# Attention and top-1 experts in one kernel: masks in two 64-row parts, a new order for attention, and the experts' first product inside that order

## The chip, the core and the metric

The kernel runs on one core of a Trainium2 chip. The metric is the device time of one execution in microseconds; the time before is the median of three runs. The engines are TensorE (PE; its weight loads are PEld), VectorE (DVE), ScalarE (ACT), GpSimd (POOL) and SyncE (SP), which starts most transfers.

## What is computed

Attention over 8 batches of 8 heads, 576 positions, head size 64, with a decay made of a running sum of logarithms, and then a mixture of 8 experts in which each token goes to one expert:

```python
scores = scale * np.matmul(q, k.transpose(0, 1, 3, 2))
cum = np.cumsum(np.log(np.clip(f, 0.0001, 1.0)), axis=-1)
scores = np.where(causal, -1e9, scores + cum[:, :, :, None] - cum[:, :, None, :])
attn = np.exp(scores - np.max(scores, axis=-1, keepdims=True))
x = (attn / (attn.sum(-1, keepdims=True) + 1e-9)) @ v        # then (4608, 512)
logits = x @ w_gate + modality_bias[modality_id]
e_idx = np.argmax(logits, axis=1)                             # gate_w: its softmax
out[mask] = gate_w[mask, None] * (np.maximum(x[mask] @ w1[e], 0.0) @ w2[e])
```

## The kernel before, in words

**Attention** takes two heads at a time, one in rows 0 to 63 of TensorE and one in rows 64 to 127: 32 pairs, four to a batch. The work of a pair p is cut into named steps. `raw`, `hi`, `lo` load and split q and k into X (the X split of GpSimd is L335). `mm` 0 to 2 compute scores for the row maxima (`max_mm`): first the causal mask is put into the PSUM bank by matmuls of a 128-row identity with a mask (L419), then come the products of X (L424) and of the decay's row (L428) with 64 rows, one matmul for each head. `mr` reduces them on VectorE (L438, L440, L443) into `mt`. `sp` transposes `mt` on TensorE (L449), `ssp` splits it on VectorE (L455, L456), `so` writes it by a transfer into Sq (L463). `s` 0 to 3 compute the shifted, masked scores (`scores`: mask L480, products L492), `e` takes their exponential on ScalarE (L502, into Pt), `h` rounds Pt to Ph on ScalarE (L513), and `r` forms the remainder Pl (L521; GpSimd, one of three on VectorE). `w` is the weighted sum with v for one head, 45 matmuls into a single bank `po` (L541 to L543), and `d` divides it on VectorE (L552 to L554) into x. `gt`, `gc`, `gm`, `ga` transpose x (L568), copy it to xT (L573), multiply by the gate (L584) and add (L590). When a batch is whole, `rt` 0 to 8 route its tokens (`route`): maximum, first expert that attains it (L602 rd, L606 and L607 rc, L610 rei), one-hot (L612, L615 roh), ranks by a small matmul, running counts (L633 acc), the destination row of every token (L640 rde), and scattering transfers of the tokens into `xs` from GpSimd (L653).

**The order of attention** is a list. `steps` describes every step with its engines, estimated durations, rings of buffers and a due time, which is the pair's number times PER plus an entry of the table DUE. `Plan.order` is a list scheduler that always takes the step that can start first, ties by due time, and the instructions of all engines are written in that order under a manual schedule. One step, `early`, makes the experts' first tables and loads the first two tiles of tokens once batch 5 is routed.

**The experts** work on tiles of 256 tokens, 21 full tiles and then half tiles (`Moe.run`). `prepare` transposes a tile's tokens (L989) and splits them into xh, xl (L991, L992). `first(t)` forms x times w1 in four groups of 24 matmuls (L1003) and splits the result into hh, hl (L1006). `second(t)` multiplies by w2 in 48 matmuls (L1014). `split_w1` and `split_w2` split the loaded weights, high half on ScalarE (L969, L976), low half on VectorE (L970, L977); L957 and L963 load them. At tile 1 `other_tables` makes the remaining tables, some 52 small VectorE instructions that follow from the last batch's counts (c_acc is L1137). Before the change all of this is written behind attention, and a scheduler orders it.

## Time and profile before

| what | us |
|---|---|
| median of three runs (lowest, highest) | 1004.14 (994.04, 1006.01) |
| the profiled execution: its time | 1013.86 |
| its span in the trace | 1012.1 |
| TensorE matmuls, busy | 927.0 (92%), 9347 instructions |
| VectorE, busy | 684.1 (68%) |
| ScalarE, busy | 537.5 (53%) |
| GpSimd, busy | 361.6 (36%) |
| mean granted TensorE clock | 0.938 |

Start times are counted from the span's start. A matmul's own duration is longer than its distance to the next, since matmuls overlap; distances of starts are what adds up. In a row with a bracket, the bracket gives the idle time ahead of the instruction and what ended it. The granted clock is a share of full speed.

### The profile page before, as it was taken

How to read it: one execution, taken by the hardware profiler on the slowest of the kernel's cores; microseconds unless marked ns; L12 is line 12 of the kernel's file. 1: busy time of each engine (PE TensorE's matmuls, PEld its weight loads, DVE VectorE, ACT ScalarE, POOL GpSimd, SP SyncE). 2: the span in 40 equal slices, each digit the busy share in tenths (PEclk: the TensorE clock that was granted, in tenths of full speed). 3: DMA queues.
4: the chain of work that ended last, by engine and by line, in shares of the span. 5: the costliest groups of instructions: out<-in, count | busy, mean ns of one | idle time of the engine just before them, and what ended most of it. 6: DMA issues, size and time to landing. Idle time of an engine off the chain costs nothing. (4 is left out here: it accounts for less than half of the span.)

```text
span 1012.1 us, 22740 instructions
## 1 busy us (share of the span) xinstructions
PE 927.0 (92%) x9347; PEld 808.8 (80%) x9347; DVE 684.1 (68%) x1173; ACT 537.5 (53%) x655; POOL 361.6 (36%) x278
## 2 busy tenths in 40 slices
PE   5999989999999899979689999999999999999792
PEld 3787778777778777768588999999999999999571
DVE  7867978686777858777547766566666666665382
ACT  2765656655756547547443444445444544544371
POOL 7454556865566474653424311111111110111010
PEclk9897999998999969989779999999999999999796
DMA  5212132332321322212302676111111441124640
GB/s 180 77 50 99 33 126 67 99 99 74 97 78 53 99 84 89 87 57 86 131 33 79 218 256 235 43 43 42 53 43 53 134 139 55 43 84 168 234 161 3
DMA packets 38276, 98.22 MB, mean 97 GB/s; under 512 B 3919, under 2 KB 4559, under 8 KB 38160
## 3 DMA queue, kind: packets, MB, share of 16 engines
q1 hardware_dynamic: 31456, 75.60, 22.5%
q0 software_dynamic: 6704, 21.02, 5.5%
q8 instruction: 79, 1.29, 0.6%
q14 instruction: 37, 0.30, 0.1%
HBM read 133.69 MB, written 21.80 MB: 154 GB/s over the span
## 5 line engine op out<-in xcount | busy, mean ns | idle before, releaser
L521 POOL TENSOR_TENSOR Pl<-Pt,Ph 128x1152 f16<-128x1152 f32 (+1 forms) x64 | 152.3, 2385 | 156.2 <-ACT Ph L513 104.4
L502 ACT ACTIVATE Pt<-ps,lnp 128x1024 f32<-128x1024 f32 (+1 forms) x128 | 117.2, 928 | 112.8 <-PE ps L492 104.8
L1017 POOL DMA_INDIRECT out_dram<-y,xg x36 | 47.4, 1316 | 349.4 <-DVE y L1016 333.1
L1003 PE MATMUL ph<-xh,w1h 128*128 128x256 f32 x576 | 164.3, 286 | 2.0 <-ACT xh L991 1.5
L1003 PE MATMUL ph<-xl,w1h 128*128 128x256 f32 x576 | 164.3, 285 | 0.0
L1003 PE MATMUL ph<-xh,w1l 128*128 128x256 f32 x576 | 164.1, 285 | 0.0
L976 ACT CAST w2h<-raw 128x1024 fp32r<-128x1024 f32 x84 | 86.6, 1050 | 115.1 <-PE py L1014 84.7
L970 DVE TENSOR_TENSOR w1l<-raw,w1h 128x1024 fp32r<-128x1024 f32 x80 | 100.9, 1265 | 58.1 <-ACT w1h L969 57.7
L977 DVE TENSOR_TENSOR w2l<-raw,w2h 128x1024 fp32r<-128x1024 f32 x84 | 100.3, 1221 | 56.5 <-ACT w2h L976 55.2
L969 ACT CAST w1h<-raw 128x1024 fp32r<-128x1024 f32 x80 | 83.3, 1048 | 95.6 <-PE ph L1003 57.8
L492 PE MATMUL ps<-X 64*128 64x288 f32 (+4 forms) x1152 | 125.8, 327 | 0.0
L1014 PE MATMUL py<-w2h,hh 128*128 128x512 f32 x312 | 121.6, 398 | 0.0
L1014 PE MATMUL py<-w2l,hh 128*128 128x512 f32 x312 | 119.7, 391 | 0.7 <-DVE w2l L977 0.7
L1014 PE MATMUL py<-w2h,hl 128*128 128x512 f32 x312 | 119.5, 392 | 0.0
L513 ACT CAST Ph<-Pt 128x1024 f16<-128x1024 f32 (+1 forms) x96 | 103.7, 1082 | 21.3 <-PE po L543 20.3
L1003 PEld LDWEIGHTS ph<-xh,w1h 128*128 128x128 f32 x576 | 111.5, 194 | 3.6 <-ACT xh L991 2.4
L1003 PEld LDWEIGHTS ph<-xl,w1h 128*128 128x128 f32 x576 | 111.7, 194 | 0.7
L541 PE MATMUL po<-vh,Ph 128*128 128x65 f16 x960 | 104.9, 202 | 7.5 <-DVE x L554 7.5
L1003 PEld LDWEIGHTS ph<-xh,w1l 128*128 128x128 f32 x576 | 111.7, 194 | 0.0
L543 PE MATMUL po<-vh,Pl 128*128 128x65 f16 x960 | 104.7, 201 | 5.0 <-issue 3.5
L542 PE MATMUL po<-vl,Ph 128*128 128x64 f16 x960 | 104.8, 200 | 1.8 <-issue 1.8
L492 PEld LDWEIGHTS ps<-X 64*128 64x128 f32 x1152 | 93.1, 196 | 13.2 <-issue 1.8
(253 smaller groups left out, 2025.7 us busy)
## 6 DMA issues: line engine op xcount, KB each, us to landing
raw<-in_w_dram SPq DMA_DIRECT2D x84, 1024.0 KB
raw<-in_qk_dram SPq DMA_DIRECT2D x32, 608.0 KB
xg<-xs SPq DMA_DIRECT2D x20, 514.0 KB
vr<-in_v_dram SPq DMA_DIRECT2D x7, 1024.0 KB
raw1b<-in_w_dram SPq DMA_DIRECT2D x4, 1024.0 KB
hxg<-xs SPq DMA_DIRECT2D x5, 257.0 KB
vr<-in_v_dram SPq DMA_DIRECT2D x2, 512.0 KB
vr<-in_v_dram SPq DMA_DIRECT2D x8, 128.0 KB
```

What stands on the lines that cost most here:

```text
L492: nc.tensor.matmul(ps[:, h, c0:c0 + w], a, b, start=(j == 0 and not masked), stop=(j == 3), skip_group_check=True)
L502: nc.scalar.activation(self.get("Pt", (p, i))[:, :, o:o + w], ps[:, :, 0:w], AF.Exp, bias=self.lnp, scale=0.125)
L513: self.nc.scalar.copy(self.Ph_t[p % 2][:, :, c], self.get("Pt", (p, i))[:, :, 0:c.stop - c.start])
L521: e.tensor_tensor(self.Pl_t[p % 2][:, :, c], self.get("Pt", (p, i))[:, :, 0:c.stop - c.start], self.Ph_t[p % 2][:, :, c], ALU.subtract)
L541: nc.tensor.matmul(o, Ph[:, c0:c0 + P], vh[:, c, hh, :], start=(c == 0), stop=False)
L542: nc.tensor.matmul(o[:, 1:65], Ph[:, c0:c0 + P], vl[:, c, hh, :], start=False, stop=False)
L543: nc.tensor.matmul(o, Pl[:, c0:c0 + P], vh[:, c, hh, :], start=False, stop=(c == ic))
L970: nc.vector.tensor_tensor(self.w1l[a], self.raw1[i][a], f32(self.w1h[a]), ALU.subtract)
L976: nc.scalar.copy(self.w2h[a], self.raw2[a])
L977: nc.vector.tensor_tensor(self.w2l[a], self.raw2[a], f32(self.w2h[a]), ALU.subtract)
L1003: nc.tensor.matmul(ph[:, i, :], w[:, k, f0:f0 + P], x[:, k, :], start=(j == 0), stop=(j == len(m) - 1))
L1014: nc.tensor.matmul(py, h[:, k, c * P:c * P + P], w[:, k, :], start=(j == 0), stop=(j == len(m) - 1))
```

## The change

1. **Masks.** The identity of 128 rows gives way to `id2`, and the masks `after` and `later` get a second plane, so that a mask is put in by matmuls of 64 rows, one for each head, as the products are. A segment wider than 64 takes two parts, one 128 columns wide and one 64 wide. A pair of heads had 20 mask matmuls and has 36.
2. **The order.** PER is 13.0 instead of 13.5, DUE has other numbers, and the step costs are given anew.
3. **Route.** L602, L606, L607 and L633 move from VectorE to GpSimd; L640 becomes three GpSimd operations.
4. **The experts' tile 0.** Loading w1 (`mw1`), tokens (`mx`) and w2 (`mw2`), splitting w1 (`ms`), `prepare` of tiles 0 and 1 (`mp`) and `first(0)` (`mf`) are steps of attention's list. For that a part of attention's buffers is closed at `mopen` and `mps`, inside the list, and the experts' tiles are opened in four pieces.

```diff
-PER = 13.5
+PER = 13.0
...
-    ('setup2',): 36.45, ('hi',): -18.87, ('lo',): -67.23, ('cum',): -14.17, ('mm', 0): -2.46, ('mm', 1): -11.48,
+    ('setup2',): 205.22, ('hi',): -34.14, ('lo',): 184.6, ('cum',): 237.26, ('mm', 0): -559.83, ('mm', 1): 5.51,
...
+        self.soon, self.soon_ps = ctx.enter_context(ExitStack()), ctx.enter_context(ExitStack())
+        pool = lambda name, bufs=1, **kw: (ctx if "side" in kw else self.soon).enter_context(tc.tile_pool(name=name, bufs=bufs, **kw))
+        self.ps_o = pool("a_o", space=PSUM, side="right")
+        self.ps_b = pool("a_b", space=PSUM, side="right")
+        self.ps_s = self.soon_ps.enter_context(tc.tile_pool(name="a_s", bufs=3, space=PSUM))
...
-        self.ident16 = t([P, P], BF16, "ident16")
-        self.later = t([P, P], BF16, "later")
-        self.after = t([P, P], BF16, "after")
-        nc.vector.tensor_copy(self.ident16, self.ident)
-        nc.gpsimd.memset(self.after, 0.0)
-        nc.gpsimd.affine_select(self.after, self.after, [[-1, P]], ALU.is_ge, -BIG, base=0, channel_multiplier=1)
+        self.id2 = t([P, 2, P], BF16, "id2")
+        self.later = t([P, 2, P], BF16, "later")
+        self.after = t([P, 2, P], BF16, "after")
+        nc.gpsimd.memset(self.id2, 0.0)
+        for x in range(2):
+            nc.vector.tensor_tensor(self.id2[:, x, 64 * x:64 * x + 64], self.ident[:, 0:64], self.ident[:, 64:P], ALU.add)
+        def mask(t, k):
+            nc.gpsimd.memset(t, 0.0)
+            for h in range(2):
+                a = t[64 * h:64 * h + 64]
+                nc.gpsimd.affine_select(a, a, [[64 * k, 2], [-k, P]], ALU.is_ge, -BIG, base=0, channel_multiplier=k)
+        mask(self.after, 1)
...
-        for h in range(2):
-            for j, (c0, w, ic, j0) in enumerate(masked):
-                n = min(w, P)
-                nc.tensor.matmul(pm[:, h, c0 + w - n:c0 + w], self.ident16, self.after[:, P - n:], start=(j == 0), stop=False,
-                                 skip_group_check=True)
+        first = True
+        for c0, w, ic, j0 in masked:
+            for x, n in ((0, P), (1, 64)) if w > 64 else ((1, 64),):
+                for h in range(2):
+                    r = slice(64 * h, 64 * h + 64)
+                    nc.tensor.matmul(pm[:, h, c0 + w - n:c0 + w], self.id2[r, x], self.after[r, x, P - n:], start=first, stop=False,
+                                     skip_group_check=True)
+                first = False
...
+        for c0, w, c, i0 in masked:
+            for x, n in ((1, P), (0, 64)) if w > 64 else ((0, 64),):
+                for h in range(2):
+                    r = slice(64 * h, 64 * h + 64)
+                    nc.tensor.matmul(ps[:, h, c0:c0 + n], self.id2[r, x], self.later[r, x, 0:n], start=first, stop=False,
+                                     skip_group_check=True)
+                first = False
...
-            nc.vector.tensor_tensor(d, lg, m.broadcast_to(s3), ALU.subtract)
+            nc.gpsimd.tensor_tensor(d, lg, m.broadcast_to(s3), ALU.subtract)
...
-            nc.vector.tensor_scalar(c, self.get("rd", b), 0.0, 8.0, ALU.is_lt, ALU.mult)
-            nc.vector.tensor_tensor(c, c, self.iota_e, ALU.add)
+            nc.gpsimd.tensor_scalar(c, self.get("rd", b), 0.0, 8.0, ALU.is_lt, ALU.mult)
+            nc.gpsimd.tensor_tensor(c, c, self.iota_e, ALU.add)
...
-            nc.vector.tensor_tensor(na, self.get("rtot", b), self.acc, ALU.add)
+            nc.gpsimd.tensor_tensor(na, self.get("rtot", b), self.acc, ALU.add)
...
-            nc.vector.scalar_tensor_tensor(de, self.get("rei", b), float(CAP), r1, ALU.mult, ALU.add)
+            e0 = sm.tile([P, NJ, 1], F32, name="re0")
+            nc.gpsimd.tensor_scalar(e0, self.get("rei", b), float(CAP), None, ALU.mult)
+            nc.gpsimd.tensor_tensor(e0, e0, r1, ALU.add)
+            nc.gpsimd.tensor_copy(de, e0)
...
+            last = [("s", n - 1, g) for g in range(4)] + [("vl", nb - 1, c) for c in range(NJ)]
+            add("mw1", (), "SP", 1.1, lambda: moe.load_w1(moe.row[0]), (), [("early",)], d, lands=2.1e6)
+            add("mopen", (), "SP", 0.0, lambda: (self.soon.close(), moe.open_left()), (), last, d)
+            for x in range(2):
+                add("mx", (x,), "SP", 0.4, lambda x: moe.load_x(x), (x,), [("mopen",)], d, lands=527e3)
+            add("mps", (), "SP", 0.0, lambda: (self.soon_ps.close(), moe.open_banks()), (), [("e", n - 1, g) for g in range(4)] + [("mopen",)], d)
+            add("mw2", (), "SP", 1.1, lambda: moe.load_w2(), (), [("mw1",), ("mopen",)], d, lands=2.1e6)
+            for q in range(4):
+                add("ms", (q,), [("ACT", 1.05), ("DVE", 1.25)], 0, lambda q: moe.split_w1(0, [q]), (q,), [("mw1",), ("mopen",)], d + q)
+            for x in range(4):
+                add("mp", (x,), [("PE", 0.6), ("ACT", 0.6), ("DVE", 0.7)], 0, lambda x: moe.prepare(x // 2, [x % 2]), (x,), [("mps",), ("mp", x - 1), ("mx", x // 2)],
+                    d + x)
+            for g in range(4):
+                add("mf", (g,), [("PE", 2.9), ("ACT", 0.75), ("DVE", 0.75)], 0, lambda g: moe.first(0, [g]), (g,),
+                    [("mp", 1), ("ms", g)], d + 1 + g, take=("ph", g), free=[("ph", g)])
...
-        self.load_w1(self.row[0])
-        self.load_w2()
-        self.split_w1()
         self.nc.gpsimd.memset(self.raw1[1], 0.0)
-        self.prepare(0)
...
-                self.first(t)
+                if t:
+                    self.first(t)
                 self.split_w1()
-                if t + 1 < FULL:
+                if 1 < t + 1 < FULL:
                     self.prepare(t + 1)
...
+        moe.open_rest()
+        moe.run(acc)
```

The places at which the instructions move, first **TensorE at a score group**, the masks ahead of 288-wide products (ident and id are the identities, later the mask, mt the maxima). Before:

```order
L449 MATMUL pb<-ident,mt 10x128
L480 LDWEIGHTS ident_162
L480 MATMUL ps<-later,ident_162 128x128
L480 LDWEIGHTS ident_162
L480 MATMUL ps<-later,ident_162 128x128
L480 LDWEIGHTS ident_162
L480 MATMUL ps<-later,ident_162 128x128
L480 LDWEIGHTS ident_162
L480 MATMUL ps<-later,ident_162 128x128
L492 MATMUL ps<-X 128x320 x6
L492 MATMUL ps<-Sq,Sk 128x320 x2
```

and after (L495 is the mask, L508 the product):

```order
L495 LDWEIGHTS id_163
L495 MATMUL ps<-later,id_163 128x128
L495 LDWEIGHTS id_163
L495 MATMUL ps<-later,id_163 128x128
L495 LDWEIGHTS id_163
L495 MATMUL ps<-later,id_163 128x64
L495 LDWEIGHTS id_163
L495 MATMUL ps<-later,id_163 128x64
L508 MATMUL ps<-X 128x288 x6
L508 MATMUL ps<-Sq,Sk 128x288 x2
```

A segment's mask is now four matmuls of 64 rows; from the mask to the products the number of rows stays the same.

Second, **a batch's route**. On VectorE before, between the reductions of the maxima (lg are the logits, rm their maximum):

```order
L438 TENSOR_REDUCE mt<-ps 128x2 x2
L590 TENSOR_TENSOR lg<-pb,lg 128x40
L600 TENSOR_REDUCE rm<-lg 128x5
L602 TENSOR_TENSOR rd<-lg,rm 128x40
L606 TENSOR_SCALAR rc<-rd 128x40
L607 TENSOR_TENSOR rc<-rc,iota_e 128x40
L440 TENSOR_REDUCE ps<-ps 128x2
L610 TENSOR_REDUCE rei<-rc 128x5
```

and on GpSimd after, between the remainders Pl and the split of X (L345):

```order
L537 TENSOR_TENSOR Pl_199<-Pt,Ph_197 128x2x576
L618 TENSOR_TENSOR rd<-lg,rm 128x40
L622 TENSOR_SCALAR rc<-rd 128x40
L623 TENSOR_TENSOR rc<-rc,iota_e 128x40
L345 TENSOR_TENSOR X<-raw,X 128x1216
L537 TENSOR_TENSOR Pl_199<-Pt,Ph_197 128x2x512
L649 TENSOR_TENSOR acc<-rtot,acc 128x8
L537 TENSOR_TENSOR Pl_198<-Pt,Ph_196 128x2x576
L657 TENSOR_SCALAR re_4845<-rei 128x5
L658 TENSOR_TENSOR re_4845<-re_4845,rr_4842 128x5
L659 CAST rde<-re_4845 128x5
```

Seven small operations of each batch have gone from VectorE's queue to GpSimd's.

Third, **the hand-over**. ScalarE after, from the last copies of the gates (xT) to the first tile's tokens (xh); raw holds weights as loaded:

```order
L589 COPY xT<-pb 128x512
L676 ACTIVATE rex<-rd 128x40
L1022 CAST w1h<-raw_78 128x4x256 x2
L1029 CAST w2h<-raw_9091 128x1024 x4
L589 COPY xT<-pb 128x128
L1022 CAST w1h<-raw_78 128x4x256 x2
L1045 CAST xh<-px_9397 128x4x128
L589 COPY xT<-pb 128x512
```

Before, the four casts of w2 came behind the tile's tokens:

```order
L573 COPY xT<-pb 128x512
L573 COPY xT<-pb 128x128
L991 CAST xh<-px_8998 128x4x128
L573 COPY xT<-pb 128x512
L991 CAST xh<-px_9160 128x4x128
L991 CAST xh<-px_9005 128x4x128
L573 COPY xT<-pb 128x128
L976 CAST w2h<-raw_8950 128x1024 x2
```

VectorE before, from the last route (rr, rde) on, the low halves of w2 at the end, the tables still to come:

```order
L638 TENSOR_REDUCE rr_8890<-rrk 128x5
L1137 COPY c_acc<-acc 128x8
L640 SCALAR_TENSOR_TENSOR rde<-rei,rr_8890 128x5
L970 TENSOR_TENSOR w1l<-raw_8935,w1h 128x4x256 x2
L1006 SCALAR_TENSOR_TENSOR hl<-ph,hh 128x512
L970 TENSOR_TENSOR w1l<-raw_8935,w1h 128x4x256
L1006 SCALAR_TENSOR_TENSOR hl<-ph,hh 128x512
L970 TENSOR_TENSOR w1l<-raw_8935,w1h 128x4x256
L1006 SCALAR_TENSOR_TENSOR hl<-ph,hh 128x512
L977 TENSOR_TENSOR w2l<-raw_8950,w2h 128x1024 x4
```

and after, the end of the 52 rows of tables (c_tabb, c_tabc, c_chb, c_chc), which begin right behind the counts of the last batch:

```order
L937 CAST c_tabb<-c_eb 1x18
L940 TENSOR_TENSOR c_chb<-c_eb 1x18
L942 TENSOR_TENSOR c_chc<-c_chc,c_okc 1x8
L943 CAST c_tabb<-c_chb 1x18
L943 CAST c_tabc<-c_chc 1x8
L1030 TENSOR_TENSOR w2l<-raw_9091,w2h 128x1024 x4
L1060 SCALAR_TENSOR_TENSOR hl<-ph,hh 128x512
L1030 TENSOR_TENSOR w2l<-raw_9091,w2h 128x1024
```

The low halves of w2 now stand behind the tables instead of ahead of them.

138 lines of the change are left out of this document (70 added, 68 removed), and 23 rows, old and new, of the table DUE.

## The prediction

> **What bounds the kernel now.** I read the windows view first, cut where the kind of work changes: attention's steady part, the hand-over, the experts.
>
> ```profile
> 25.00:487.00 462.00, 429.83 (x6157) 361.91 (x6155) 347.72 (x728) 288.65 (x343) 263.20 (x158) 0.93 0.25 81
> 487.00:558.00 71.00, 58.54 (x451) 53.46 (x450) 42.11 (x87) 27.36 (x39) 26.12 (x24) 0.78 0.24 84
> 558.00:1012.00 454.00, 425.45 (x2665) 383.99 (x2664) 275.94 (x326) 214.39 (x267) 53.97 (x41) 0.97 0.32 111
> ```
>
> The columns are the stretch, its length, the busy time of PE (TensorE's matmuls), PEld (its weight loads), DVE (VectorE), ACT (ScalarE) and POOL (GpSimd) with the instruction count, the granted clock, and DMA's share and GB/s. TensorE is the fullest engine in all three. In attention it idles 462 - 429.8 = 32.2 us, and a clock of 0.93 costs it another 0.07 x 462 = 32.3 us, so at most 64.5 us can be had there without taking work away. The experts' stretch runs at 0.97, is untouched by the change, and stays. So two things count: TensorE's work and losses in attention, and the 71 us of hand-over.
>
> What TensorE waits for in attention, from the waits view (microseconds in total, times, longest):
>
> ```profile
> PE po L541 <- DVE x L554: 6.9, 4, 5.1
> PE pb L449 <- DVE roh L615: 4.8, 2, 3.1
> PE po L543 <- issue: 3.5, 5, 1.2
> PE pb L568 <- DVE lg L590: 3.2, 3, 1.1
> PE pb L449 <- DVE mt L443: 2.5, 3, 0.8
> PE pb L449 <- DVE rei L610: 2.2, 1, 2.2
> PE ps L480 <- DVE mt L438: 2.2, 3, 1.1
> ```
>
> Six of the seven rows name VectorE: 6.9 + 4.8 + 3.2 + 2.5 + 2.2 + 2.2 = 21.8 us. Rows on L449 are the transpose that turns the row maxima into shifts. VectorE is busy only 347.7 of 462 us, so it isn't short of time on the whole; it is late at certain places. The timeline of one of them:
>
> ```profile
> 220.72 2.63 DVE L606 TENSOR_SCALAR rc<-rd 128x40 f32<-128x40 f32 x1
> 223.38 2.07 DVE L607 TENSOR_TENSOR rc<-rc,iota_e 128x40 f32<-128x40 f32 x1
> 220.54 2.77 POOL L335 TENSOR_TENSOR X<-raw,X 128x1216 fp32r<-128x1216 f32 x1
> 223.27 2.13 POOL L521 TENSOR_TENSOR Pl<-Pt,Ph 128x1024 f16<-128x1024 f32 x1
> 227.28 0.27 PE L449 MATMUL pb<-ident,mt 128*10 128x128 f32 x1 [1.66 <-DVE roh L615]
> 220.00:240.00 20.00, 18.34 (x247) 15.62 (x249) 16.14 (x32) 9.29 (x12) 8.31 (x5) 0.74 0.11 34
> ```
>
> Two of the route's operations on 40 elements take 2.63 and 2.07 us on VectorE, each ending where a big GpSimd operation ends (220.54 + 2.77 = 223.31; 223.27 + 2.13 = 225.40). The reductions behind them on VectorE come late, TensorE waits 1.66 us, and the 20 us that hold this run at a clock of 0.74. The lost clock follows the stalls.
>
> The Trainium skill, "SBUF — State Buffer", section "Who interferes with whom", says that a VectorE instruction with two SBUF inputs and a GpSimd instruction that reads SBUF exclude each other for the whole instruction, whichever came first. The second row fits that; the first has one tensor input and was held as long, which the section ties to a two-port mode.
>
> **The masks.** A timeline around one mask group of 64 columns, and the matmuls on both sides:
>
> ```profile
> 204.06 0.47 PE L492 MATMUL ps<-X 64*128 64x192 f32 x6
> 204.37 0.28 PE L492 MATMUL ps<-Sq,Sk 64*128 64x192 f32 x2
> 204.58 0.34 PE L419 MATMUL ps<-after,ident 128*128 128x64 bf16 x4
> 204.86 0.30 PE L424 MATMUL ps<-X 64*128 64x64 f32 x2
> 204.99 0.28 PE L428 MATMUL ps<-Sk,Cq 64*128 64x64 f32 x2
> 11.32 0.53 PE L428 MATMUL ps<-Sk,Cq 64*128 64x192 f32 x2 [2.52 <-DMA Sk<-chl]
> ```
>
> Read start to start: six 192-wide matmuls take 0.31, so a pair takes 0.10, but the pair at 204.37 takes 0.21 up to the mask: the step from 64 rows to 128 costs some 0.1 us, an estimate from these rows. The order has 462 such steps back and forth on TensorE up to the experts' first product; in the changed order they are 325, because a mask of 64 rows stands among products of 64 rows. That is 137 x 0.1 = -13.7 us. Against it stand more matmuls: 20 masks a pair of heads become 36, that is 18 twos whose halves lie on different rows. Now the four masks take 0.28, of which 0.1 is the step back, so 0.045 each and some 1.0 us a pair of heads. A two costs at least one such mask (0.04, the halves wholly side by side) and at most 0.09 (the 64-wide f32 two at 204.86 took 0.13 with what the change of operand added): 0.7 to 1.6 us. I take the middle, 1.16, since neither row is nearer: +0.15 x 32 = +5. Together **-9**, with ends of -23 and +5. The setup's few more operations for the masks' parts count nothing: TensorE waits for a transfer of Sk until 11.32 us anyway; without that cover they would cost under 1 us, at 0.2 to 0.5 us each on GpSimd.
>
> **The route's operations on GpSimd.** VectorE sheds these, and they cost:
>
> ```profile
> L606 DVE TENSOR_SCALAR rc<-rd 128x40 f32<-128x40 f32 x7 | 7.5, 1068 | 0.1
> L640 DVE SCALAR_TENSOR_TENSOR rde<-rei,rr 128x5 int32<-128x5 f32 x6 | 6.0, 992 | 0.2
> L602 DVE TENSOR_TENSOR rd<-lg,rm 128x40 f32<-128x40 f32 x7 | 5.8, 824 | 0.2
> L607 DVE TENSOR_TENSOR rc<-rc,iota_e 128x40 f32<-128x40 f32 x7 | 5.1, 734 | 0.2
> L633 DVE TENSOR_TENSOR acc<-rtot,acc 128x8 f16<-128x8 f32 x6 | 3.0, 500 | 0.0
> 516.22 0.18 DVE L606 TENSOR_SCALAR rc<-rd 128x40 f32<-128x40 f32 x1
> POOL xs L653 <- DVE rde L640: 23.9, 3, 8.0
> ```
>
> The sum over the window 100 to 480 us is 27.4 us in 33 instructions; at the 0.18 us of the row at 516.22, where GpSimd stands idle, they would be 6. So 21 us of VectorE are blocked time, at places where the max reductions queue behind. On GpSimd one batch now has seven small operations. No row shows them there: between 0.18 us each (VectorE unhindered) and 2.63 (held up as above), 1.3 to 18 us a batch. I take 1 us each, near the mean rows above, 7 us a batch on an engine that has 462 - 263 = 199 us free. In its queue they stand between the low halves of the weights (Pl), which the weighted products wait for. By itself I cost the move at nothing: the cover is TensorE's work between a pair's last score and its first weighted product, which the new order raises from 5.8 us at the least (typically 9) to 10.8 (typically 14), counted along the order at the durations of the trace.
>
> **The new order.** The same count for the other places where TensorE waited: between the last max product and the transpose, at the least 1.7 us before and 3.55 now; between two weighted products, whose single bank VectorE must free, 0.2 before and some 1.2 to 1.7 now. A wait in the list above ends when its lateness, 0.8 to 3.1 us beyond the old cover, fits into 1.9 us more of it. Of the six VectorE rows, 4.8, 3.2, 2.5, 2.2 and 2.2 mostly fit, and the 6.9 row only in part (one of its four is 5.1): I take three quarters of 21.8, 16.4 us, half of the idle time. The clock's 32.3 us follow the stalls, so half of these too, 16.5. Together **-33**. The ends: nothing (new places stall as much as the old ones: with fewer idle us, VectorE is busy for 348 of some 425), and 21.8 + 32.3 = -54.
>
> **The hand-over.** T0 is the end of the last score product, 486.6.
>
> ```profile
> 486.32 0.28 PE L492 MATMUL ps<-Sq,Sk 64*128 64x192 f32 x2
> 490.00:500.00 10.00, 2.49 (x18) 2.21 (x18) 7.55 (x7) 0.96 (x2) 6.06 (x4) 0.68 0.71 243
> 500.00:520.00 20.00, 18.02 (x150) 17.20 (x148) 6.15 (x22) 7.27 (x12) 0.00 (x0) 0.50 0.01 1
> 503.13 2.30 PE L584 MATMUL pb<-wg,xT 128*128 128x8 f32 x10 [0.35 <-ACT xT L573]
> 512.53 1.01 PE L1003 MATMUL ph<-xh,w1h 128*128 128x256 f32 x3 [0.46 <-ACT xh L991]
> L976 ACT CAST w2h<-raw 128x1024 fp32r<-128x1024 f32 x84 | 86.6, 1050 | 115.1 <-PE py L1014 84.7
> 515.52 0.20 DVE L590 TENSOR_TENSOR lg<-pb,lg 128x40 f32<-128x40 f32 x1 [2.31 <-PE pb L584]
> 517.75 0.23 DVE L618 TENSOR_REDUCE rtot<-roh 128x8 f32<-128x40 f16 x1
> 561.61 0.16 DVE L871 TENSOR_TENSOR c_kb<-c_kb,c_baseb 1x18 f32<-1x18 f32 x1
> 563.45 0.15 DVE L890 CAST c_tabc<-c_chc 1x8 int32<-1x8 f32 x1
> 557.85 0.48 PE L1014 MATMUL py<-w2h,hh 128*128 128x512 f32 x1
> ```
>
> Before: the experts' first product starts at 512.53, T0 + 25.9, and the second product of tile 1 at T0 + 71.2. The change writes the first product into attention's list, but on ScalarE four casts of w2 now stand ahead of the xT copy that TensorE's next route and gate steps need. They wait for w2's load, which stands on SP's queue behind the last pair's shift loads, w1's and the loads of x (nothing of attention stands behind it there). Its 2.1 MB at 243 GB/s take 8.6 us, so it lands some 11 us after T0; the casts end at 11 + 4 x 1.05 = 15.2; two casts of w1 follow, 2.1; and from there the gates of a pair, the transposes and their copies run as between 503.13 and 512.53, 9.4 us, with 0.8 for a second transposed half. The first product starts at T0 + 27.5: **+1.6**. Then TensorE has the two halves of first products and tile 1's, with the last two pairs' gates among them, and comes to tile 0's second product. That needs w2l, and on VectorE the four w2l stand behind 52 rows of the other tables, which wait for the counts of the last route: 3.0 us of route (515.52 to 517.75 with its end and GpSimd's hops), 0.9 for four counting rows at 0.2, the tables (21 of them from 561.61 to 563.45, so 0.09 each, some with 144 elements up to 0.3) 6.1, and 1.3 for the first w2l. That is **+11.3** of TensorE's time, where before w2l stood ahead of the tables. Some 4 us of work that now stands behind T0 has left the steady part: **-4**. In sum **+9**. The ends: if w2 has landed when ScalarE comes to it, the first product starts at about T0 + 10 and the tables are done in its shade, 10 - 25.9 - 4 = -20; if the clock stays at 0.50 behind the second stop as in 500 to 520, where TensorE was 90% busy, 24 us more at half speed are +12, so +21.
>
> The Trainium skill, "TensorE: Matmul & The Clock Gate", Part 1, says that half clock ends after one busy window of about 3.4 us. The row of 500 to 520 differs: 0.50 for 20 us with TensorE 90% busy. By that rule the stop would cost an estimated 1.7 us in clock, and the upper end would be +11.
>
> **The sum**, against the profiled execution (span 1012.1, time 1013.86): -9 - 33 + 9 = -33, 980.9. That execution lies 1% above the median of the runs, 1004.14; the same ratio, 0.990, gives **971 us**.
>
> **Rivals.** First, that the losses stay: the new order has other tight places, and only masks and hand-over count, -9 + 9 = 0, so 1004. For it speaks that VectorE's share of the time rises, and that the "issue" row and the 5.1 us wait aren't touched by covers; against it, that the waits sit at few places whose cover about doubled. Second, on the other side, **GpSimd's queue**: the seven small operations wait in order for VectorE's part of the route, and the Pl behind them wait with them. The row of 8.0 us is such a wait of GpSimd's queue for the route. Past 10.8 us of lateness, the smallest cover, TensorE stands. With the low halves late by 18 us at the upper price above, it loses 18 - 10.8 = 7.2 us in each of seven batches, 50, and the clock with it 6: -33 + 56 = +23, 1027. Against it: GpSimd is free 43% of the time and the small operations stand where it mostly waited. By the Trainium skill's "SBUF — State Buffer", section "Who interferes with whom", the moved operations, which read SBUF, would be held in their turn by VectorE's long two-input ones. No run here has shown that direction yet. Third, **the hand-over runs through**: w2 is loaded soon enough, -20 instead of +9, which gives -62, 951.9, so 943.
>
> **How the numbers follow.** The forecast has 0.60, the losses that stay 0.23, GpSimd's queue 0.07, the smooth hand-over 0.10. The forecast's own range, from the mask's and the order's ends, is 955 to 988. The range wanted runs from the smooth hand-over's middle to a little over the first rival's, 943 to 1008. It leaves out half of the third rival, a quarter of the first and the second, 0.18. A measurement of this kernel tells about 2% from no change, 984 to 1024: faster is 0.87 of the forecast and the third rival, 0.62; same is the rest of the forecast and nearly all of the first rival, 0.30; slower the second and a little of the first, 0.08.
>
> **What would show it.** In the profile after: attention up to its last score product ending near 440 to 450 us with a clock of 0.96 or more; the L438/L440/L443 reductions without a 2 us neighbour; fewer than 20 us of TensorE waiting in it. Behind it, a stop of TensorE of some 15 us ahead of the first expert product with ScalarE waiting for the w2 load, and one of some 11 us ahead of tile 0's second product with VectorE in the tables. The masks: less than 1.3 us a pair, and no 0.2 us after the last score product ahead of a mask. It is wrong if attention's steady part keeps its 32 us of idle time, or if the waits for Pl grow past 20 us.

## The result and the profile after

The changed kernel takes 1010.6 us (median of 20 runs, 1006.6 to 1016.4), the kernel before 1007.3 us (20 runs, 994.0 to 1020.5): a ratio of 1.0067, with a 95% interval of 1.0043 to 1.0092. The forecast was 971 us and a range of 943 to 1008; the change brought no gain there. The profiled execution took 1011.8 us with a span of 1010.0 us, where that of before had 1012.1. The windows view of the changed kernel, cut at the same events as before (the last score product at 474.5, its end at 474.6, and the second product of tile 1 at 551.1), with the same columns:

```profile
25.00:474.50 449.50, 409.41 (x6547) 352.70 (x6545) 349.26 (x673) 281.48 (x333) 271.35 (x195) 0.91 0.25 80
474.50:551.00 76.50, 58.36 (x532) 53.11 (x531) 43.99 (x122) 31.11 (x45) 32.41 (x46) 0.84 0.26 95
551.00:1010.00 459.00, 430.35 (x2667) 383.72 (x2665) 276.76 (x302) 214.69 (x269) 51.94 (x41) 0.98 0.32 110
```

Attention ends 12.0 us earlier (474.6 against 486.6), the hand-over is 5.2 us longer (76.5 against 71.3 us), and the rest, which the change was not to touch, is 4.7 us longer (458.9 against 454.2): -12.0 + 5.2 + 4.7 = -2.1, the difference of the spans. The point is in the first row. TensorE's work there, busy time by clock, fell from 429.8 x 0.93 = 400 to 409.4 x 0.91 = 373 us, 27 us less. But the idle time rose from 32.2 to 40.1 us and what the clock costs from 32.3 to 0.09 x 449.5 = 40.5 us. So 16 of the 27 us were lost again. The waits view of the changed kernel, attention from 25 us on, TensorE's largest:

```profile
PE pb L462 <- DVE z L568: 7.8, 5, 1.6
PE ps L495 <- DVE ps L453: 6.0, 6, 1.1
PE pb L600 <- issue: 5.4, 11, 0.9
PE ps L508 <- issue: 3.9, 5, 1.2
```

Two things are new in it. More than half of the waits for VectorE, which had many names before, now stand in two rows that come about once in every batch (five and six times, up to 1.6 and 1.1 us). And there are stops that no releaser explains ("issue"): 13.7 us in TensorE's rows up to T0, against 5.3 before. The next two timelines show one of each.

**The stop in every batch.** VectorE, GpSimd and TensorE of the changed kernel around 245 us, then the windows behind it:

```profile
242.67 2.58 DVE L628 TENSOR_TENSOR roh<-iota_e,rei 128x40 f32<-128x40 f32 x1
245.16 0.75 DVE L453 TENSOR_REDUCE ps<-ps 128x2 f32<-128x576 f32 x1
245.83 1.49 DVE L631 TENSOR_TENSOR roh<-roh,valid 128x40 f16<-128x40 f32 x1
247.50 0.75 DVE L456 TENSOR_REDUCE mt<-ps 128x2 f32<-128x578 f32 x1
242.41 2.77 POOL L345 TENSOR_TENSOR X<-raw,X 128x1216 fp32r<-128x1216 f32 x1 [1.41 <-ACT X L339]
245.15 2.11 POOL L537 TENSOR_TENSOR Pl<-Pt,Ph 128x1024 f16<-128x1024 f32 x1
245.97 0.26 PE L495 MATMUL ps<-later,id 64*128 64x128 bf16 x4 [1.13 <-DVE ps L453]
248.39 0.37 PE L462 MATMUL pb<-ident,mt 128*10 128x128 f32 x1 [1.55 <-DVE z L568]
```

```profile
246.00:249.00 3.00, 1.45 (x15) 1.00 (x16) 2.90 (x6) 0.74 (x1) 1.46 (x2) 0.84 0.62 208
249.00:252.00 3.00, 3.00 (x54) 2.72 (x53) 2.25 (x8) 0.91 (x2) 0.00 (x0) 0.59 0.03 7
```

L628 and L631 make the one-hot of the chosen expert; the change left both on VectorE. L628 ends at 245.25, where GpSimd's L345 ends (242.41 + 2.77 = 245.18); L631 ends at 247.32, where L537 ends (245.15 + 2.11 = 247.26). The reductions L453 and L456 stand behind them, TensorE waits 1.13 us for L453 and 1.55 us for z (L568), the operation right behind L456, and its next 3 us run at a clock of 0.59 although it is busy all the time. This is the picture on which the prediction rested, with other operations in it. The Trainium skill, "SBUF — State Buffer", section "Who interferes with whom", has a VectorE instruction with two SBUF inputs and a GpSimd instruction that reads SBUF shut each other out: L628 and L631 are such instructions, and the trace agrees, with 2.58 us for an operation that takes 0.20 in the kernel before where GpSimd stands idle (L612 at 517.28 us).

**The stops without a releaser.** TensorE's rows of the changed kernel from 261 us on, and 2 us windows there:

```profile
261.68 0.89 PE L600 MATMUL pb<-wg,xT 128*128 128x8 f32 x4 [0.83 <-issue]
...
264.54 0.24 PE L495 MATMUL ps<-later,id 64*128 64x64 bf16 x2 [0.45 <-issue]
```

```profile
258.60:260.60 2.00, 1.24 (x28) 1.01 (x24) 1.19 (x2) 1.24 (x2) 1.78 (x3) 1.00 0.95 285
260.60:262.60 2.00, 1.02 (x7) 1.05 (x6) 0.00 (x0) 0.00 (x0) 1.56 (x5) 0.77 1.07 396
262.60:264.60 2.00, 1.03 (x8) 0.67 (x8) 0.00 (x0) 0.00 (x0) 1.97 (x2) 0.50 1.02 315
264.60:266.60 2.00, 2.00 (x15) 1.48 (x17) 1.31 (x6) 0.60 (x1) 1.36 (x1) 0.50 0.16 45
```

For 6 us TensorE works half of the time, the profile names nothing that it waits for, and the DMA engines are full (0.95 to 1.07): v's load and the scatter of the tokens (xs) run together there. The clock falls to 0.50 and stays there in the next window.

Full DMA engines and v's load aren't needed for it, though. In the window of the last of attention's six scatters only the scatter's transfers run from 438 us on, at a DMA share of 0.57, and it holds six of the 25 stops (2.5 of the 13.7 us). In the kernel before, all eight stops (5.3 us) stand beside a scatter alone. First the window of the changed kernel, then one scatter instruction and the first stop behind it before:

```profile
436.80:442.60 5.80, 3.36 (x57) 2.76 (x55) 1.56 (x3) 2.21 (x3) 5.13 (x8) 1.00 0.57 201
```

```profile
182.37 0.90 POOL L653 DMA_INDIRECT xs<-x,rde  x1 [0.23 <-issue]
183.00 0.19 PE L542 MATMUL po<-vl,Ph 128*128 128x64 f16 x1 [0.74 <-issue]
```

**The hand-over.** TensorE's rows of the changed kernel at its ends and its stops, and ScalarE's casts:

```profile
474.32 0.28 PE L508 MATMUL ps<-Sq,Sk 64*128 64x192 f32 x2
496.38 0.58 PE L1057 MATMUL ph<-xh,w1h 128*128 128x256 f32 x1 [0.68 <-ACT xh L1045]
526.67 0.21 PE L639 MATMUL pb<-roh,tri 128*128 128x40 f16 x1 [2.39 <-DVE roh L631]
535.29 0.80 PE L1068 MATMUL py<-w2l,hh 128*128 128x512 f32 x1 [7.25 <-DVE w2l L1030]
```

```profile
482.37 1.98 ACT L1022 CAST w1h<-raw 128x1024 fp32r<-128x1024 f32 x2
484.25 3.88 ACT L1029 CAST w2h<-raw 128x1024 fp32r<-128x1024 f32 x4
```

The casts of w2 follow the casts of w1 without a wait: the load had landed, and the first product starts at T0 + 21.8, where the prediction had 27.5. The stop ahead of the second product of tile 0 is there: 7.25 us for the tables and the first w2l, near the predicted 6.1 + 1.3 (8.3 with the counting rows).

### The profile page after: what moved, and what is told of

The parts are those of the page before. It is cut to its first block, busy times and chain, and to the rows that moved or that the text cites. A ratio compares the mean times of both kernels' runs of the same rounds, so it can differ in the third digit from the quotient of the medians.

```text
span 1010.0 us, 23820 instructions
## 1 busy us (share of the span) xinstructions
PE 912.2 (90%) x9859; PEld 800.2 (79%) x9859; DVE 688.9 (68%) x1134; ACT 537.0 (53%) x655; POOL 376.7 (37%) x337
## 5 line engine op out<-in xcount | busy, mean ns | idle before, releaser
L537 POOL TENSOR_TENSOR Pl<-Pt,Ph 128x1152 f16<-128x1152 f32 (+1 forms) x64 | 149.0, 2333 | 93.3 <-ACT Ph L529 87.4
L1071 POOL DMA_INDIRECT out_dram<-y,xg x36 | 44.9, 1247 | 346.8 <-DVE y L1070 319.1
L1023 DVE TENSOR_TENSOR w1l<-raw,w1h 128x1024 fp32r<-128x1024 f32 x80 | 97.2, 1224 | 63.9 <-ACT w1h L1022 63.9
L508 PE MATMUL ps<-X 64*128 64x288 f32 (+4 forms) x1152 | 132.8, 338 | 5.5 <-issue 3.9
L345 POOL TENSOR_TENSOR X<-raw,X 128x1216 fp32r<-128x1216 f32 x31 | 87.6, 2827 | 76.2 <-ACT X L339 76.1
L557 PE MATMUL po<-vh,Ph 128*128 128x65 f16 x960 | 109.3, 205 | 5.5 <-DVE x L570 5.0
L559 PE MATMUL po<-vh,Pl 128*128 128x65 f16 x960 | 109.1, 204 | 1.8 <-issue 1.8
L558 PE MATMUL po<-vl,Ph 128*128 128x64 f16 x960 | 109.0, 203 | 0.8 <-issue 0.7
```

The source lines that it names most:

```text
L345: e.tensor_tensor(X[:, 1], self.get("raw", p), f32(X[:, 0]), ALU.subtract)
L508: nc.tensor.matmul(ps[:, h, c0:c0 + w], a, b, start=(j == 0 and not masked), stop=(j == 3), skip_group_check=True)
L537: e.tensor_tensor(self.Pl_t[p % 2][:, :, c], self.get("Pt", (p, i))[:, :, 0:c.stop - c.start], self.Ph_t[p % 2][:, :, c], ALU.subtract)
L557: nc.tensor.matmul(o, Ph[:, c0:c0 + P], vh[:, c, hh, :], start=(c == 0), stop=False)
L558: nc.tensor.matmul(o[:, 1:65], Ph[:, c0:c0 + P], vl[:, c, hh, :], start=False, stop=False)
L559: nc.tensor.matmul(o, Pl[:, c0:c0 + P], vh[:, c, hh, :], start=False, stop=(c == ic))
```

## The experiments

The kernels of one group ran on the same chip beside runs of the kernel before, and chips differ: the kernel before takes 1007 us on the recorded chip, 1017 on another (its runs there spread from 1001 to 1032, so ratios to it are less sure there) and 1023 to 1027 on the rest, which are four. So each run is compared with its own chip. Which chip the recorded one was is not known; it may be the one with 1017. T0 is again the end of the last score product.

**Both kernels on a second chip.** No edit: the changed kernel, and the kernel before with a profile.

> The changed kernel as it is, beside the kernel before on one chip. In the runs so far its steady part took 42 us longer in one trace (last score product at 474) than the same instructions in the run with the tables made later (432), and only the first of the two shows the 13.7 us of stops without a releaser. Theory (those stops come from transfers that land slower on that chip, not from the program's order): without such stops here, 975 to 980 and a ratio to before of 0.95 to 0.97; with them, 1005 to 1012. Rival (the later tables shifted something else in the steady part): 1005 to 1012 without any such stop.

> The kernel before as it is, for a trace on the same chip as the others of this call. Theory: TensorE's waits are those of the first trace (VectorE 22 us, issue 5 us), and the time differs from it by the granted clock behind them; rival: other waits, so that the two traces of before are no measure for each other.

The changed kernel takes 974.7 us there against 1026.8: 0.951 [0.945, 0.957]. It has T0 at 434.8 (474.6 on the recorded chip), and from T0 on nearly the same: second product of tile 1 at T0 + 78.1 (76.5), rest 459.1 (458.9). The difference of 39.8 us in T0 is all in attention. Its windows at the same place of the program, where v's load and the scatter run together:

```profile
244.00:246.00 2.00, 2.00 (x25) 1.69 (x26) 1.05 (x4) 0.73 (x2) 1.56 (x5) 1.00 1.08 406
246.00:248.00 2.00, 2.00 (x59) 1.79 (x57) 0.39 (x2) 1.48 (x3) 1.98 (x2) 1.00 1.02 331
25.00:434.70 409.70, 385.12 (x6535) 334.12 (x6533) 349.37 (x670) 281.10 (x333) 271.73 (x195) 0.95 0.28 89
```

The transfers fill the DMA engines as on the recorded chip (1.02 to 1.08), and TensorE doesn't stop. Over attention it idles 24.6 us here (40.1 there), and the clock costs 20.5 us (40.5 there): 35.5 of the 39.8 us. The kernel before has its own trouble on this chip, its T0 is 510.1 (486.6 there). VectorE, GpSimd and TensorE of that profile:

```profile
186.55 12.42 DVE L521 TENSOR_TENSOR Pl<-Pt,Ph 128x1024 f16<-128x1024 f32 x1
186.29 6.80 POOL L521 TENSOR_TENSOR Pl<-Pt,Ph 128x1024 f16<-128x1024 f32 x3
193.06 2.74 POOL L335 TENSOR_TENSOR X<-raw,X 128x1216 fp32r<-128x1216 f32 x1
195.77 2.11 POOL L521 TENSOR_TENSOR Pl<-Pt,Ph 128x1024 f16<-128x1024 f32 x1
200.33 0.16 PE L369 MATMUL pb<-ident,a 3*1 3x3 f32 x1 [6.51 <-DVE lg L590]
```

VectorE's share of Pl ends at 198.97, 1.1 us after the last of five GpSimd operations in a row (195.77 + 2.11 = 197.88), and TensorE stops for 6.51 us. In the first profile of before, VectorE got in after one GpSimd operation at this place, and it was the next GpSimd operation that waited (3.32 us, 2.1 otherwise):

```profile
188.83 2.75 DVE L521 TENSOR_TENSOR Pl<-Pt,Ph 128x1024 f16<-128x1024 f32 x1
```

**The masks alone**, in the old order: the mask part of the diff, applied to the kernel before.

```diff
-        for h in range(2):
-            for j, (c0, w, ic, j0) in enumerate(masked):
-                n = min(w, P)
-                nc.tensor.matmul(pm[:, h, c0 + w - n:c0 + w], self.ident16, self.after[:, P - n:], start=(j == 0), stop=False,
...
+        for c0, w, ic, j0 in masked:
+            for x, n in ((0, P), (1, 64)) if w > 64 else ((1, 64),):
+                for h in range(2):
...
```

> The kernel before with only the masks changed to two 64-row parts; its order and due times stay. Theory (the masks save TensorE 20 to 27 us, and the new order gives most of it back): 15 to 27 us faster than before, a pair's mask groups at 0.09 us for four, 0.12 for six, 0.18 for eight matmuls. Rival (attention is bound by the chain through VectorE and ScalarE, so what TensorE saves turns into waits under any order): within 5 us of before, TensorE's waits in the steady part up from 32 to over 50 us.

1007.0 against 1026.9 us, 0.979 [0.974, 0.984]: 20 us faster, inside the first theory's bounds. Its window, and that of before on the second chip:

```profile
25.00:488.60 463.60, 407.13 (x6604) 352.97 (x6601) 371.76 (x724) 285.57 (x341) 262.85 (x158) 0.90 0.24 80
```

```profile
25.00:510.10 485.10, 439.89 (x6155) 369.25 (x6152) 373.21 (x728) 288.34 (x343) 261.31 (x158) 0.89 0.23 77
```

Work by clock is 407.1 x 0.90 = 366 against 439.9 x 0.89 = 392: 25 us less, not 9. Part of it was lost here too: the idle time is 56.5 us against 45.2 (the two profiles come from two chips on which before takes 1027).

**128-row masks in the new order**: the reverse edit on the changed kernel.

> The changed kernel with the masks of 128 rows put back; its order, route and hand-over stay. Theory (the masks gave about as much as they gave in the order before, 20 us of TensorE's time): 993 to 1003 where the changed kernel takes 975. Rival (the new order waits for VectorE and ScalarE, so TensorE's work is not what counts): within 6 us of 975.

972.1 us, 0.945 [0.940, 0.950], and T0 at 434.7, within 0.1 us of that of the changed kernel on this chip. Here the rival was right: in the new order, with the one-hot at its place, the 64-row masks are worth nothing. Its window and one wait:

```profile
25.00:434.70 409.70, 402.23 (x6065) 336.98 (x6064) 338.59 (x675) 283.31 (x333) 271.78 (x195) 0.98 0.27 89
```

```profile
PE pb L453 <- DVE z L556: 1.7, 5, 0.3
```

TensorE's work by clock is 394 us instead of 366, 28 more, and its idle time is 7.5 us instead of 24.6, its clock 0.98 instead of 0.95. The wait that took 7.8 us takes 1.7, that of 6.0 us is gone, and all rows that name VectorE sum to 7.2 us instead of 23.2. The masks' work was the cover of VectorE's late reductions; where it is taken away, TensorE waits.

**The one-hot later**: the two steps with L628 and L631 moved in the list to just ahead of the step that needs them.

```diff
-            for s in self.steps(early, moe).order():
+            order = self.steps(early, moe).order()
+            for b in range(7):
+                for j in (2, 3):
+                    at = lambda j: [s["name"] for s in order].index(("rt", b, j))
+                    s = order.pop(at(j))
+                    order.insert(at(8), s)
+            for s in order:
```

> The changed kernel with the route's one-hot steps of batches 0 to 6 moved later in attention's list, behind the maxima's reductions and ahead of the normaliser. Theory (the one-hot operations, held by GpSimd for 2.6 and 1.5 us, make the reductions late): the two stops of 1.1 and 1.6 us a batch and the clock of 0.6 to 0.8 behind them vanish, 8 to 20 us faster than the changed kernel. Rival (TensorE is early there and waits for whatever comes last): the stops move to the rank product or the next reduction, time within 3 us.

> The changed kernel with the one-hot steps later, a second time; it took 954 on a chip on which the changed kernel had no stop without a releaser. Theory (that gain and those stops are independent): 954 again on such a chip, and 980 to 992 on one with them, 18 to 25 us below the changed kernel's 1009. Rival (the gain needs a chip without them): over 1000 there.

954.1 against 1026.9 us, 0.928 [0.923, 0.934], and on a further chip 954.4 against 1027.4, 0.928 [0.922, 0.934]: 20 us below the changed kernel on the second chip. The profile of the first: window and the two operations.

```profile
25.00:414.00 389.00, 376.91 (x6536) 326.47 (x6534) 333.56 (x670) 281.30 (x333) 272.47 (x195) 0.97 0.29 95
```

```profile
225.93 0.63 DVE L628 TENSOR_TENSOR roh<-iota_e,rei 128x40 f32<-128x40 f32 x1
226.59 0.20 DVE L631 TENSOR_TENSOR roh<-roh,valid 128x40 f16<-128x40 f32 x1
```

The same TensorE work as in the changed kernel (376.9 x 0.97 = 366 us) ends 20.7 us earlier. L628 takes 0.63 us, both waits of every batch are gone (the largest single one left is 2.8 us, for x), idle time is 12.1 us (24.6) and the clock costs 11.7 us (20.5). That the one-hot's place in the order held TensorE up is shown.

**The one-hot later with 128-row masks**, on a chip that has the stops without a releaser, beside the changed kernel.

> The changed kernel with the masks of 128 rows put back and the one-hot steps later. With the one-hot steps at their place the masks were worth nothing (972 with 128 rows, 975 with two parts): TensorE's time saved ended as waits of 1.1 and 1.6 us a batch for reductions. Theory (that stop alone eats them): without it the masks count again, so 965 to 973 here, some 12 to 20 us above the 954 with both. Rival (attention is bound elsewhere, and TensorE's work does not count): 951 to 958.

> The changed kernel as it is, a third time. Theory (the stops without a releaser belong to the chip that the first comparison ran on): on one of the chips used since, no such stop and 972 to 978; on that first one, where before takes about 1007, stops of over 10 us and 1005 to 1015. Rival (they come and go on any chip): stops here with before at about 1027.

The changed kernel takes 1008.7 us there, 0.995 [0.991, 0.999] of before; with the one-hot later and 128-row masks it is 1000.0, 0.987 [0.980, 0.994]. Both profiles have the stops (12.2 and 9.0 us). Since the masks' share wasn't run apart on this chip, it says only that 9 us are to be had there by the two. Whether the 64-row masks count again once the one-hot is later, which was the question, stays untested: no chip ran both masks with the one-hot later.

**The route's five operations back on VectorE**, in the new order.

```diff
-            nc.gpsimd.tensor_tensor(d, lg, m.broadcast_to(s3), ALU.subtract)
+            nc.vector.tensor_tensor(d, lg, m.broadcast_to(s3), ALU.subtract)
...
```

> The changed kernel with the route's five operations back on VectorE, at the same places of attention's list. Theory (small operations on VectorE are held up by GpSimd's long ones and the reductions queue behind them): VectorE's time in these lines goes up by 15 to 25 us over seven batches, TensorE's waits for VectorE rise by 5 to 20 us, and the kernel is 10 to 30 us slower than the changed one on the same chip. Rival (the move changes nothing that TensorE waits for): within 3 us.

978.1 us, 0.953 [0.947, 0.960]: 3.4 us more than the changed kernel on this chip (974.7), T0 at 442.0. VectorE spends 19.7 us on the five (they are seven operations on GpSimd), but TensorE's waits for it rise by only 3.2 us. The move is worth 3 us, far from the 27 us that these operations had held VectorE for; the theory of 10 to 30 is wrong.

**The tables late**: the other tables' rows behind w2l, with 32 bytes of padding ahead of w2h; and the same with the one-hot later and the padding ahead of hh.

```diff
-OTHERS = 1
+OTHERS = 2
...
+        one([P, 8], F32, "pad")
```

> The changed kernel with the other tables made at tile 2 instead of tile 1, so that the four w2l stand ahead of them on VectorE, and with 32 bytes of padding ahead of w2h. Theory (the stop of 7.2 us ahead of tile 0's second product is the tables): that stop falls under 2 us and the time by 5 to 9 us against the changed kernel's 1010.6. Rival (the tables only take the place of another wait, for w2 itself): the stop stays above 5 us and the time within 2 us. On the second product's matmuls, which start every 235 ns and before every 229: if the address of w2h modulo 64 bytes sets it, they go to 229 and 5 us more are gained; if not, they stay at 235.

> The changed kernel with both edits: the one-hot steps later, and the other tables at tile 2; beside them 32 bytes of padding ahead of hh. Theory (the two stops lie in different stretches, so the gains add): 18 us and 5 us below the changed kernel on the same chip, 946 to 951 where that has no issue stops. Rival (the tables' stop hides another wait): no more than 18 us. If the address of hh modulo 64 bytes sets the second product's distance, it falls from 233 to 227 ns and another 5 us are gained.

The first takes 972.8 us, 0.947 [0.942, 0.952], with its second product at T0 + 71.1, 7 us earlier than in the second run of the changed kernel; but its rest is 463.9 instead of 459.1. The second takes 952.5, 0.930 [0.924, 0.937]. Its waits view names where the time went:

```profile
PE ph L1064 <- DVE hl L1067: 3.8, 1, 3.8
```

The tables now hold VectorE when tile 2 wants its hidden values. From T0 to the end the first has -7.0 + 4.8 = -2.2 us against the changed kernel, the second -6.3 + 7.5 = +1.2 against the one-hot kernel (its T0 is 2.7 us earlier): the stop is moved by a tile, not taken away. The padding was to try whether an address makes the second product slow, one of whose three groups reads, in before and in the changed kernel (groups view from T0 on):

```profile
L1014 PE MATMUL py<-w2h,hl 128*128 128x512 f32 x312 | 119.5, 392 | 0.0
```

```profile
L1068 PE MATMUL py<-w2h,hl 128*128 128x512 f32 x312 | 121.2, 397 | 0.0
```

Neither padding moved it.

**The old hand-over**: tile 0's first product written behind attention again.

```diff
-            add("mw1", (), "SP", 1.1, lambda: moe.load_w1(moe.row[0]), (), [("early",)], d, lands=2.1e6)
...
+        for t in range(2):
+            self.load_x(t)
...
+        self.prepare(0)
```

> The changed kernel without the experts' steps in attention's list; loading, splitting, preparing and the first product of tile 0 are written behind it, as before, and ordered by the scheduler. Theory (the hand-over in the list costs some 5 us, the tables' stop): 965 to 973 where the changed kernel takes 975. Rival (the steps in the list save what they were made for, an early first product): 978 to 995.

983.8 us, 0.955 [0.950, 0.959], 9 us more than the changed kernel, but not by what it was to show. Its largest wait behind attention:

```profile
PE px L1031 <- DMA xg<-xs: 14.3, 2, 13.0
```

The tiles of x open later than in the kernel before, and TensorE waits 14.3 us for the tokens, which it didn't there. Taken off in full that would put it some 5 us below the changed kernel, as the theory has it; but as the old hand-over in the new order it isn't faithful, and that comparison stays open.

**What the stops without a releaser are.** Five kernels. The scatter 25 places later in the list (with w2h and w2l placed elsewhere); v's load of 1 MB doubled by a transfer beside it; v's load 14 places later; v's load left out from the third batch on, alone and with the one-hot later (these two leave that load out, attend with batch 1's v and route other tokens, so their experts' part isn't comparable). In this order:

```diff
+                i = [s["name"] for s in order].index(("rt", b, 6))
+                order.insert(i + 25, order.pop(i))
...
+        e.dma_start(self.vx, self.vin[b, 0:512, :])
...
+                i = [s["name"] for s in order].index(("v", b))
+                order.insert(i + 14, order.pop(i))
...
+        if b < 2:
+            e.dma_start(self.vr[:, c0:n, :], self.vin
...
```

> The changed kernel with the scatter of batches 0 to 4 moved 25 entries later in attention's list, behind v's load instead of beside it, and with w2h and w2l placed behind three other pools. Theory (v's load and the scatter together starve TensorE, whose stops there have no releaser in the profile): the stops called issue fall from 13.7 to under 7 us and the clock in that third of a batch recovers, 5 to 15 us faster than the changed kernel. Rival (the stops belong to the products of that place or to the load alone): issue stops within 3 us of 13.7, time within 3 us. The second product's matmuls: 229 ns if the place of w2h and w2l among the other tiles sets it, else 235.

> The changed kernel with a second transfer of 1 MB, from memory to memory, beside each load of v. In the first trace of the changed kernel TensorE's instructions come late (13.7 us of stops without a releaser) while v's load and the scatter fill the transfer engines for 7 us; two later traces of other runs show the same transfers and no such stop. Theory (instructions are fetched through the same engines, and the stops come when they are full for longer than what is fetched ahead): stops called issue appear, 10 us or more in sum, and the kernel gets 20 to 60 us slower than 975. Rival (the stops had nothing to do with transfers): none appear, and the time stays within 8 us of 975, apart from waits for v itself.

> The changed kernel with v's load of batches 2 to 7 moved 14 entries later in attention's list, so that it begins when the scatter is nearly done. Theory: where the stops without a releaser appear in the changed kernel they come from both transfers together, and here they fall to under 5 us, 10 to 30 us faster; where they don't appear, the time is within 4 us of the changed kernel's, or slower by what TensorE or VectorE waits for v. Rival: the stops stay with the transfers apart.

> The changed kernel without the 1 MB load of v for batches 2 to 7 (only the last 64 rows are loaded; the other rows keep batch 1's values, so that part of the computation is left out). Where the changed kernel shows stops of TensorE without a releaser, they stand in the 7 us in which v's load and the scatter run together. Theory (the full transfer engines cause them): the stops fall under 3 us and the kernel takes 970 to 980 on any chip. Rival (they come from the scatter, or from the chip whatever is transferred): over 8 us of such stops and over 995 on a chip where the changed kernel takes 1005 to 1012. On a chip without the stops both expect 970 to 980, and the run tells nothing.

> The changed kernel with the one-hot steps later and without the 1 MB load of v for batches 2 to 7 (that part of the computation is left out). On a chip on which stops without a releaser appear in the changed kernel (before at 1000 to 1020 there): theory (v's load beside the scatter causes them): under 3 us of them, 945 to 955; rival (the scatter alone, or the chip): over 6 us and over 975. On a chip without them (before at about 1027) both expect 945 to 955.

The scatter later gives 1007.0 us, 0.980 [0.975, 0.985], on a chip where a kernel that differs from the changed one only in the tables takes 972.8. It costs 34 us by another mechanism. The low halves Pl wait in GpSimd's queue, as in the prediction's second rival, but behind the five instructions of the scatter itself (6.3 us, 144.24 to 150.50) and not behind the route's small operations:

```profile
PE po L559 <- POOL Pl L537: 20.0, 5, 4.0
```

v doubled gives 990.7, 0.965 [0.957, 0.972]: 16 us more than the changed kernel, with one stop of 1.1 us. So full DMA engines, on a chip without the stops, don't make stops of 10 us and more. v later gives 1013.2, 1.007 [1.003, 1.011], on the chip with the stops; the load went some 4 us later, but the scatter some 3 us too, and they still ran together, so the edit didn't part them (16.0 us of stops). The stops came at other products. First and last of a row of six, 0.71 us apart:

```profile
198.50 0.19 PE L557 MATMUL po<-vh,Ph 128*128 128x65 f16 x1 [0.48 <-issue]
...
202.07 0.23 PE L559 MATMUL po<-vh,Pl 128*128 128x65 f16 x1 [0.51 <-issue]
```

They follow the transfers in time and not a kind of product. v left out gives 967.5, 0.940 [0.934, 0.947], and with the one-hot later 945.7, 0.923 [0.915, 0.930]; neither has a stop. On the first of these chips the one-hot kernel with v's load has none either, and on the other no kernel with it ran, so the two don't tell whether v's load matters.

The other profiles do. Five have such stops (before and the changed kernel on the recorded chip; the third run of the changed kernel, v later, and the one-hot with 128-row masks on the other), 106 in all up to T0. Every one lies between the first instruction of a batch's scatter on GpSimd and the end of its packets, 8 to 10 us a batch. In all five some stand beside the scatter alone, while v's loads away from a scatter, at DMA shares of 0.60 to 0.76, have none. So on these chips the stops go with the scatter, and v's load beside it isn't needed. No run took the scatter out, and the same scatter makes none on the four other chips.

**Pl wholly on GpSimd**, in the kernel before: does the shut-out of VectorE's share explain its 1027 us?

```diff
-        e = self.nc.vector if i == 1 else self.nc.gpsimd
+        e = self.nc.gpsimd
```

> The kernel before with the third of Pl that VectorE makes put on GpSimd. Theory (in the second trace of before VectorE's Pl is locked out for up to 12.4 us by GpSimd operations that follow each other without a gap, 45 us in sum over 32 against 16 in the first trace, which is why it took 1027 us there and 1007 elsewhere): no VectorE operation above 4 us, 1000 to 1015 where before takes 1027. Rival (GpSimd becomes late itself with 69 us more): TensorE waits for Pl by over 15 us, no gain or slower.

1024.1 us, 0.998 [0.994, 1.002]: no gain. VectorE has no operation above 3 us any more, and GpSimd is late instead:

```profile
PE po L543 <- POOL Pl L521: 15.7, 10, 2.5
```

## Why the prediction was wrong

**Where it failed: the steady part.** The prediction put -9 for the masks and -33 for the order, -42 in all (-46 with the work moved), and T0 came 12.0 us earlier. Two steps failed, and a loss that no step had came on top.

*The order's term, three quarters of 21.8 us.* VectorE's waits did not shrink: all of TensorE's rows that name it, from 25 us to T0, sum to 22.9 us before and 23.9 after. I took it that a wait ends when the cover grows by 1.9 us, and counted cover for the old waits alone. But the new order put the one-hot, which the change leaves on VectorE, beside GpSimd's L345 and L537 in every batch. The prediction had blamed just this neighbourhood (rc held for 2.63 and 2.07 us) and had checked only the five operations that left; L615, now L631, already stood in its list of waits with 4.8 us. Moving the two steps gave 20 us (954 against 975), shown on two chips. The cover that the prediction counted for the order was there all the same: with the 128-row masks put back the new order leaves 7.2 us of these rows on the second chip, with the one-hot where it was. It was the change's own masks that took it away.

*The masks at -9.* The mechanism was right and the size too small: work by clock fell by 27 (400 to 373), 25 (392 to 366) and 28 us (394 to 366) in three pairs of profiles, beyond the -23 that was the far end. The term that was mis-sized is the pair of half-masks side by side, the "two" of the prediction, taken at 1.16 us for 18: six 64-row masks now start within 0.13 us, 0.022 each:

```profile
270.75 0.29 PE L431 MATMUL ps<-after,id 64*128 64x64 bf16 x6
270.88 0.28 PE L437 MATMUL ps<-X 64*128 64x64 f32 x2
```

That is 0.043 for a two, about the lower bound, and 0.8 us for 18: some -21 in the prediction's own sum. The 4 to 7 us beyond it aren't traced. And it was added to the order's gain as if the two were independent. They aren't: less work is less cover. In the old order the masks gave 20 us, in the new one nothing (972.1 us with 128 rows, 974.7 with 64).

*What no step had.* On the recorded chip TensorE stops for some 14 us without a releaser while a scatter runs, most of them with v's load beside it, and its clock falls to 0.50 there. The "issue" row of 3.5 us in before's waits, which is the same thing, was seen and left where it was. On the second chip the same kernel has none of these stops, T0 is 434.8 and the time 975, near the forecast of 971, but for a part by chance: the VectorE waits that were to go are there (23.2 us), and the larger saving by the masks makes up for them. The ratio of 0.951 owes part to the kernel before, whose T0 is 23.5 us later on that chip than on the recorded one, with 21.1 us of waits at the places of the 12.42 us operation. What the stops cost, with the clock, is about the 35.5 us of idle time and clock by which the two profiles of the changed kernel differ; that all of it comes from the stops is argued, not shown. They come with the scatter, on the recorded chip and on the one with 1017 us and not on the four others, and twice v's transfer doesn't make them there. Why a chip has them stays open.

**The first rival** said that the losses stay, 1004 us, since the new order has other tight places. That is what happened, and 1010.6 lies 7 us from it: not for reasons of the order alone, though. It had 0.23.

**The hand-over, +9.** Of this, -4 lies ahead of T0; the stretch behind T0 was put at 1.6 + 11.3 = +12.9 and came out at +5.2. The first product starts at T0 + 21.8 instead of 27.5, because w2 had landed when ScalarE came to it, and the casts ended at T0 + 13.5, not 15.2; from there on 8.2 us were enough, not 12.3. That is the condition of the third rival, but the gain was small, because the last gates still stand between. Of the +11.3 us of stop ahead of the second product, the route took 2.4 (3.0 predicted), and counting rows, tables and the first w2l 7.25 (8.3): 9.6 in all, the mechanism right and the size near.

**The route's move at nothing** held: 3.4 us. The warning rule on GpSimd's side didn't decide either; waits for Pl, which were to show it, aren't among the changed kernel's rows of 0.4 us or more. That Pl can hold TensorE up from GpSimd's queue is shown by the scatter kernel (20.0 us), there behind the scatter.

**The rest, held to stay,** is 4.7 us longer: the second products take 397 ns in place of 392, which is 1.7 us over the 312 of one group and some 5 us over the three. Neither of the two paddings nor another place for w2 changed it. It stays with the 128-row masks (rest 459.7), with the route back on VectorE (459.0) and with the old hand-over (458.7), and the masks alone don't bring it (453.9); the cause is open.

**The best version** is the changed kernel with the one-hot later: 954 us, 0.928 of before on two chips (952.5 with the tables late as well, a difference that the tables don't explain). It was not run on a chip with the stops; with 128-row masks it took 1000 us there.

## What to carry to other kernels

Work that is taken off the bound engine is also cover for whoever is late, so its gain and that of a new order can't be added: look first for what will end last once it is gone. When small operations are moved because a neighbour on another engine holds them, follow every operation of that kind that stays, to its new neighbours in the order; here two that stayed cost 20 us. And run both kernels on more than one chip before a profile's waits are called the kernel's: here the same pair gave 1.007, 0.995 and 0.951. When several things run at a stop, look for a place where one of them runs alone: here before's own profile had it.

## What the runs showed of the hardware

Chips differ by some 4 per cent: the changed kernel took 975 us on one and 1011 and 1009 in two other groups of runs, with the same transfers, and what the profiles show beside it are stops of TensorE of 0.2 to 1.2 us, some every 0.71 us, which all lie within a scatter, at DMA shares from some 0.3 up to full. A VectorE operation with two SBUF inputs can be held for more than one GpSimd operation: 12.42 us, five in a row, where 2.75 us was the time when it got in after one. And six bf16 masks of 64 rows, in pairs on both halves of the rows, start within 0.13 us.
